# A gated mix of linear attention and eight experts: more rooms for the sums of the second layer's weights, and another order of the steps of the queries

## The chip, the cores and the metric

The kernel runs on one core of one Trainium2 chip. The metric is the device time of one execution in microseconds (us), the median of several runs. Times of single instructions come from one profiled execution.

## The reference, cut to what matters

```python
x = A_x                                             # 1 x 2048 x 512
g = sigmoid((x * gate_w).sum(-1, keepdims=True))
a = A_ref(x, A_wqkv, A_wo)
b = B_ref(x, B_w_gate, B_w1, B_w2)
return g * a + (1 - g) * b

def A_ref(x, wqkv, wo):                             # 32 heads of 16
    q, k, v = split_heads(x @ wqkv)
    phi = lambda t: where(t > 0, t + 1, exp(t)) + 1e-6
    pq, pk = phi(q), phi(k)
    kv = einsum("bhsd,bhse->bhde", pk, v)
    z = einsum("bhsd->bhd", pk)
    num = einsum("bhqd,bhde->bhqe", pq, kv)
    den = einsum("bhqd,bhd->bhq", pq, z)[..., None] + 1e-6
    return merge_heads(num / den) @ wo

def B_ref(x, w_gate, w1, w2):                       # 8 experts, hidden width 1792, all 8 are taken
    gates = softmax(x @ w_gate)
    return sum(gates[:, e] * (silu(x @ w1[e]) @ w2[e]) for e in range(8))
```

## The kernel before, in words

Every float32 operand of a matmul is split in a high part (a copy by ScalarE into the type the matmul rounds to) and a low part (VectorE: the value minus the high part). `mm3` (L56) multiplies high by high, high by low and low by high: lines 57, 58 and 59 are these three matmuls everywhere. `act_copy` (L61) is the copy by ScalarE; all such copies have line 62. `split` (L224) is the copy and the subtraction, one after the other. Both matmuls of an expert are computed by a scheme of seven products of halves in place of eight, so sums and differences of blocks of the inputs, of the weights and of the hidden values are made first.

The program has three stages.

**Keys.** The keys' features and the sums with the values are gathered over all 2048 rows. It ends with `normaliser`, `drain`, `state`, `gates` and `fold`, which give the matrix `wph`, `wpl` (state times `wo`, high and low).

**Queries.** The rows are in four blocks s = 0 to 3 of 512; each block has four slices c = 0 to 3 of 128 features.
- `q_proj(s, c)` (L414) makes 12 matmuls into a bank "a" of PSUM (there are two), then `phi`: an exponential on ScalarE (L320) and two steps of VectorE (L321, L322). Then it splits the result into `un`.
- `q_sums(s)` (L429), after the four slices of a block, makes 12 matmuls into bank "b" (one bank), a copy by ScalarE, one reciprocal of 32 x 512 by VectorE (L436), and the split into `rh`.
- `q_norm(s, c)` (L440) spreads the reciprocals over the features by two matmuls into bank "c" (one bank), multiplies by them on VectorE (L445), and splits the product into `hl`.
- `a_out(s, c)` (L449) makes 12 matmuls of `hl` with `wph` and `wpl` into four banks "dn"; after the last slice ScalarE copies them out (L461), and they are stored.
- `x_sums(p, step)` (L515) makes, for half p of the rows, four sums of blocks of x on VectorE (steps 0 to 3, 128 x 1024 each) and splits them (steps 4 to 7). For p = 1 the parts are stored to DRAM (`xstash`).

The blocks overlap: block s is projected while block s - 2 is normalised and put out. Near the end the first group of expert weights is loaded (`m.load`) and prepared (`m.prep`).

**Experts.** A group g is 256 of the hidden units of an expert; there are 112 groups (two halves of the rows, eight experts, seven groups each). `up(g, k, ...)` (L634), k = 0 to 6, makes the seven products of a group, six matmuls each, into banks "a", "b", "c". `prep(g + 1, k)` (L130) at the same time prepares the next group's weights: the first layer's go into tiles `o`; the second layer's (sums included) go into tiles `ws`, four to a group and two rooms in all, and are stored to DRAM (`w2stash`, seven stores a group, L183 and L158). The raw weights `rm` come in four loads a group into two rooms (L117, L120). From step u = LAG = 44 on, `tick(n)` (L803) adds the second layer: six matmuls more in each step. Its hidden operands are tiles `ho` (five rooms), its weights come back from `w2stash`.

The order on each engine is the order of the code: nothing is scheduled by a tool. An instruction waits on its engine until its inputs are there and its room is free, and everything behind it on that engine waits with it. Loads and stores are issued in order on SP's queue, but for some on GpSimd's.

The whole order of the queries is at L537 to L585.

Of the kernel before, what the change touches and what calls it, by code (L numbers as in the profile page):

```python
# [16 lines left out]
P = 128  # L17
# [19 lines left out]
def f32(ap):  # L37
    return ap.bitcast(F32)
# [57 lines left out]
def weights(m):  # L96
# [5 lines left out]
    m.ORDER = ("P1", "P7", "P2", "P4", "P6", "P5", "P3")  # L102
    raw, ops, ws = {}, {}, {}
    m.ops = ops


    def raw_tile(name):
# [22 lines left out]
    def prep(g, step):  # L130
# [12 lines left out]
        def low(i, src):  # L143
            o = ops[g][i][0]
            v.tensor_sub(two(o, 1), src, f32(two(o, 0)))  # L145

        def high2(n, src):
            if both:
                w = ws[g, n] = o_tile(f"ws{g}_{n}", "ws", 2, D)
                act_copy(two(w, 0), src)  # L150

        def low2(n, src, *prods):
            if both:
# [13 lines left out]
        elif step == 1:  # L167
# [2 lines left out]
            act_copy(o[:, 0], r[:, 1, 1, 0])  # L170
            ops[g][6] = o, 0
            if both:
                w = ws[g, 0] = o_tile(f"ws{g}_0", "ws", 2, D)
                act_copy(w[:, 0, :HALF], r[:, 0, 0, 1])
            high2(1, r[:, :, 1, 1])
        elif step == 2:
            o = ops[g][6][0]
# [28 lines left out]
def attention(m):  # L206
# [207 lines left out]
    def q_proj(s, c):  # L414
        tb = TBO[s]
        cs = slice(c * P, (c + 1) * P)
        ps = m.ps_tile(f"q{s}{c}", "a")
        for k in range(KT):
            nc.tensor.matmul(ps, wqh[:, k, cs], xk(0, tb, k), start=(k == 0), stop=False)
            nc.tensor.matmul(ps, wqh[:, k, cs], xk(1, tb, k), start=False, stop=False)  # L420
        for k in range(KT):
            nc.tensor.matmul(ps, wql[:, k, cs], xk(0, tb, k), start=False, stop=(k == KT - 1))
        d = pq[s, c] = sf_tile(f"pq{s}{c}") if s in (0, 3) else scr[:, (s - 1) * KT + c, :]
        phi(d, ps)
        u = un[s, c] = o_tile(f"un{s}{c}")
        split(d, u[:, 0], u[:, 1])


    def q_sums(s):  # L429
        ps = m.ps_tile(f"dn{s}", "b")[:NH, :]  # L430
        for c in range(KT):
            u = un.pop((s, c))
            mm3(ps, zc[:, 0, c, :], zc[:, 1, c, :], u[:, 0], u[:, 1], c == 0, c == KT - 1)
        r = hid.tile([NH, TB], F32, name=f"r{s}", tag="r", bufs=1)
        nc.scalar.activation(r, ps, AF.Copy, bias=1e-6)
        v.reciprocal(r, r)  # L436
        rec[s] = hid.tile([NH, 2, TB], F32R, name=f"rh{s}", tag="rh", bufs=2)
        split(r, rec[s][:, 0], rec[s][:, 1])

    def q_norm(s, c):  # L440
        ps = m.ps_tile(f"n{s}{c}", "c")
        for j in range(2):
            nc.tensor.matmul(ps, spread[:, c, :], rec[s][:, j], start=(j == 0), stop=(j == 1))
        d = pq.pop((s, c))
        v.tensor_mul(d, d, ps)  # L445
        h = hl[s, c] = hl_tile(f"hl{s}{c}")
        split(d, h[:, 0], h[:, 1])

    def a_out(s, c):  # L449
        h = hl.pop((s, c))  # L450
# [64 lines left out]
    def x_sums(p, step):  # L515
        a, b = raw[2 * p], raw[2 * p + 1]
        b11, b21, b12, b22 = a[:, :2], a[:, 2:], b[:, :2], b[:, 2:]
        if step == 0:
            v.tensor_sub(b11, b12, b11)
        elif step == 1:  # L520
            v.tensor_sub(b12, b22, b12)
        elif step == 2:
            v.tensor_sub(b22, b22, b11)
        elif step == 3:
            v.tensor_sub(b21, b21, b22)
        else:
            i, r = ((1, b11), (3, b22), (5, b12), (6, b21))[step - 4]
            if p == 0:
                XO[0][i] = [x_tile(f"t{i}{c}") for c in "hl"]
                split(r, *XO[0][i])  # L530
            else:
                h, lo = hl_tile(f"t{i}h"), hl_tile(f"t{i}l")
                split(r, h, lo)
                for c, t in enumerate((h, lo)):
                    nc.sync.dma_start(m.xstash[step - 1, c], f32(t).rearrange("p k t -> p (k t)"))

    q_proj(0, 0)  # L537
    y_acc(NT - 1)
    normaliser()
    drain()  # L540
    q_proj(0, 1)
    state()
    gates()
    q_proj(0, 2)
    q_proj(0, 3)
    wph, wpl = fold()
    for c in range(KT):
        q_proj(1, c)
        if c == 0:
            q_sums(0)  # L550
        x_sums(1, c)
    for s in (2, 3):
        for c in range(KT):
            q_proj(s, c)
            if c == 0:
                q_sums(s - 1)
            q_norm(s - 2, c)
            if s == 2:
                x_sums(1, 4 + c)
            else:  # L560
                x_sums(0, c)
            if c > 0:
                a_out(s - 2, c - 1)
        if s == 2:
            load_x(0), load_x(1)
        a_out(s - 2, KT - 1)
    q_norm(2, 0)
    q_sums(3)
    for c in range(KT):
        if c:  # L570
            q_norm(2, c)
        x_sums(0, 4 + c)
        if c > 0:
            a_out(2, c - 1)
        if c == 2:
            m.load(0)
    q_norm(3, 0)
    a_out(2, KT - 1)
    m.load(1)
    for c in range(KT):  # L580
        if c + 1 < KT:
            q_norm(3, c + 1)
        m.prep(0, 2 * c)
        a_out(3, c)
        m.prep(0, 2 * c + 1)  # L585

    XO[0][0], XO[0][2], XO[0][4] = X[0, 0], X[0, 1], X[1, 1]
    nc.gpsimd.memset(m.ident, 1.0)
# [6 lines left out]
def experts(m):  # L595
# [132 lines left out]
    def high(n):  # L728
        if 0 <= n < NTICK:
# [1 line left out]
            if n % 6 == 5:  # L731
                h = m.xpool.tile([P, 2, TB], F32R, name=f"ho{n}", tag="xs", bufs=2)
            else:
                h = hp.tile([P, 2, TB], F32R, name=f"ho{n}", tag="ho", bufs=5)
            act_copy(h[:, 0], t[SRC[prod]])
            hop[n] = h, t[SRC[prod]]

# [140 lines left out]
    for u in range(LAG + NTICK):  # L878
# [107 lines left out]
```

## Time and profile before

| what | us |
|---|---|
| median of 3 runs (2427.65 to 2429.86) | 2428.75 |
| the profiled execution's own time | 2427.99 |
| its span, first to last instruction | 2426.2 |
| TensorE busy (PE) | 2384.3 |
| its weight loads (PEld), beside PE | 1956.8 |
| VectorE busy (DVE) | 1807.9 |
| ScalarE busy (ACT) | 1369.1 |
| GpSimd busy (POOL) | 135.0 |

Rows of the profile name the engine, the line, the operation, then output and inputs by the program's names, and the shape. `<-` behind an idle time names what ended it. "PEclk" or "granted clock" is TensorE's clock as a share of full speed. Matmuls overlap, so their pitch is read from their starts and not from their durations.

### The profile page before, as it was taken

The page shows a single profiled execution, that of the slowest core. Times are in us where ns is not written, and L with a number is a line of the kernel's source. Part 1 is how long each engine was busy: PE and PEld are TensorE (multiplying, and loading weights), DVE is VectorE, ACT ScalarE, POOL GpSimd, SP SyncE. Part 2 cuts the span into 40 slices and gives each one's busy share as a digit, 9 for nine tenths or more (in the row PEclk, how much of TensorE's full clock was granted, in tenths as well). Part 3 has the DMA queues.
Part 4 walks back from the last instruction along what each step waited for, and adds up shares of the span by engine and source line. Part 5 has one row for each costly group of instructions (what it writes and reads, how often), then busy time and mean ns, then how long its engine had stood idle before and what let it go on. Part 6 is the DMA issues. An engine that isn't in the chain of part 4 may idle for free.

```text
span 2426.2 us, 31298 instructions
## 1 busy us (share of the span) xinstructions
PE 2384.3 (98%) x10627; PEld 1956.8 (81%) x10627; DVE 1807.9 (75%) x3055; ACT 1369.1 (56%) x2545; POOL 135.0 (6%) x173
## 2 busy tenths in 40 slices
PE   8988899999999999999999999999999999999998
PEld 7865678888888888888888888888888888888887
DVE  6666688888888888888887667666766766666757
ACT  4343666666666666666655555555555555555543
POOL 2100100000000000000000000000000000000011
PEclk9999999999999999999999999999999999999999
DMA  4422788879888888889886544455454544445456
GB/s 146 149 96 96 233 272 261 284 255 280 260 267 271 264 278 260 269 266 284 263 261 236 147 157 155 161 165 161 148 160 134 150 139 142 142 142 156 134 171 225
DMA packets 295984, 487.66 MB, mean 201 GB/s; under 512 B 22416, under 2 KB 214032, under 8 KB 294672
## 3 DMA queue, kind: packets, MB, share of 16 engines
q1 hardware_dynamic: 278480, 453.09, 55.9%
q0 software_dynamic: 17344, 32.58, 7.8%
q8 instruction: 83, 1.36, 0.2%
q14 instruction: 77, 0.63, 0.1%
HBM read 334.52 MB, written 151.06 MB: 200 GB/s over the span
## 4 chain that ended last, share of the span: by engine, by line
PE 92%; DVE 3%; DMA 2%; ACT 1%; issue 1%; SPq 1%; DVEq 0%; ACTq 0%
PE p L57 15%; PE p L58 15%; PE p L59 15%; PE a L57 8%; PE a L59 8%; PE a L58 8%; PE c L58 4%; PE c L57 4%; PE c L59 4%; PE b L58 2%; PE b L57 2%; PE b L59 2%; PE g L329 1%; DMA w2stash<-ws 1%; DVE r L436 0%
## 5 line engine op out<-in xcount | busy, mean ns | idle before, releaser
L57 PE MATMUL p<-ho,w 128*128 128x512 f32 x1568 | 611.0, 390 | 1.5 <-DVE k L798 0.7
L58 PE MATMUL p<-ho,w 128*128 128x512 f32 x1568 | 610.0, 389 | 0.0
L59 PE MATMUL p<-ho,w 128*128 128x512 f32 x1568 | 610.0, 389 | 0.0
L741 DVE TENSOR_TENSOR ho<-s,ho 128x512 fp32r<-128x512 f32 x784 | 537.5, 687 | 60.8 <-ACT ho L62 58.3
L62 ACT ACTIVATE ho<-s 128x512 fp32r<-128x512 f32 x784 | 487.3, 622 | 18.9 <-PE p L59 12.7
L57 PEld LDWEIGHTS p<-ho,w 128*128 128x128 f32 x1568 | 294.3, 188 | 64.8 <-ACT p L62 1.8
L59 PEld LDWEIGHTS p<-ho,w 128*128 128x128 f32 x1568 | 294.4, 188 | 61.2
L58 PEld LDWEIGHTS p<-ho,w 128*128 128x128 f32 x1568 | 294.3, 188 | 60.8
L62 ACT ACTIVATE o<-rm 128x512 fp32r<-128x512 f32 x448 | 255.5, 571 | 149.5 <-PE a L59 124.6
L624 ACT ACTIVATE s<-s 128x512 f32<-128x512 f32 x224 | 141.7, 633 | 286.2 <-DVE s L683 208.2
L145 DVE TENSOR_TENSOR o<-rm,o 128x512 fp32r<-128x512 f32 x336 | 230.5, 686 | 14.4 <-ACT o L62 13.8
L683 DVE TENSOR_TENSOR s<-c,s 128x512 f32<-128x512 f32 x112 | 77.3, 690 | 168.1 <-PE c L59 164.5
L62 ACT ACTIVATE ws<-rm 128x256 fp32r<-128x256 f32 x224 | 126.7, 572 | 87.3 <-DMA w2stash<-ws 74.6
L690 DVE TENSOR_TENSOR s<-a,s 128x512 f32<-128x512 f32 x112 | 77.4, 691 | 74.1 <-PE a L59 73.5
L155 DVE TENSOR_TENSOR ws<-rm,ws 128x512 fp32r<-128x512 f32 x168 | 115.3, 687 | 20.5 <-ACT ws L62 18.9
L624 ACT ACTIVATE s<-b 128x512 f32<-128x512 f32 x112 | 67.3, 600 | 104.8 <-PE b L59 91.4
L62 ACT ACTIVATE s<-a 128x512 f32<-128x512 f32 x112 | 66.8, 597 | 91.2 <-PE a L59 91.2
L178 DVE TENSOR_TENSOR o<-rm,o 128x256 fp32r<-128x256 f32 x112 | 47.2, 422 | 64.2 <-ACT o L62 63.9
L775 POOL DMA_DIRECT2D acct<-c x28 | 24.2, 864 | 1093.5 <-DVE c L771 650.1
L62 ACT ACTIVATE s<-c 128x512 f32<-128x512 f32 x112 | 66.7, 596 | 26.7 <-PE c L59 26.7
L713 DVE TENSOR_TENSOR s<-s,s 128x512 f32<-128x512 f32 x112 | 77.0, 688 | 0.0
L722 DVE TENSOR_TENSOR s<-s,s 128x512 f32<-128x512 f32 x112 | 77.0, 687 | 0.0
(334 smaller groups left out, 4471.7 us busy)
## 6 DMA issues: line engine op xcount, KB each, us to landing
w<-w2stash SPq DMA_DIRECT2D x392, 512.0 KB, 4.3
w2stash<-ws SPq DMA_DIRECT2D x392, 256.0 KB, 4.7
rm<-wm SPq DMA_DIRECT2D x336, 256.0 KB, 4.8
wb<-wgtd SPq DMA_DIRECT2D x16, 512.0 KB, 5.7
x<-xT SPq DMA_DIRECT2D x7, 1024.0 KB, 6.2
acct<-c POOLq DMA_DIRECT2D x28, 256.0 KB, 5.7
acct<-d POOLq DMA_DIRECT2D x28, 256.0 KB, 5.7
acct<-k POOLq DMA_DIRECT2D x26, 256.0 KB, 5.4
```

Source lines behind the costliest of these rows:

```text
L57: nc.tensor.matmul(ps, wh, xh, start=start, stop=False, skip_group_check=True)
L58: nc.tensor.matmul(ps, wh, xl, start=False, stop=False, skip_group_check=True)
L59: nc.tensor.matmul(ps, wlo, xh, start=False, stop=stop, skip_group_check=True)
L62: nc.scalar.activation(dst, src, AF.Copy)
L145: v.tensor_sub(two(o, 1), src, f32(two(o, 0)))
L155: v.tensor_sub(two(w, 1), src, f32(two(w, 0)))
L624: nc.scalar.activation(dst, src, AF.Silu)
L683: v.tensor_add(sn[g, 2], bank[g, "c"], sn[g, 2])
L690: v.tensor_add(sn[g, 3], bank[g, "a"], sn[g, 3])
L713: v.tensor_sub(t12, t22, t12)
L722: v.tensor_sub(t21, t21, t11)
L741: v.tensor_sub(h[:, 1], s, f32(h[:, 0]))
```

## The change

Six things are changed.

1. `q_proj` no longer splits. The copy (`q_high`) and the subtraction (`q_low`) are functions of their own, so are those of `q_norm` (`n_high`, `n_low`) and those of the x splits (`x_high`, `x_low`); the order of the queries places them one by one.
2. The reciprocal of a block is made in four quarters of 32 x 128 (`q_rec`), one in each slice of the next block; the split of it follows as `q_rec_split`.
3. `q_norm` takes bank "c" for even slices and bank "b" for odd ones.
4. The x sums and splits stand at other places: two sums of half 1 are made during block 0, the splits of half 1 during the first two slices of block 2; the sums of half 0 during block 3, its splits from there into the remainder. The order of the splits is 3, 5, 1, 6 in place of 1, 3, 5, 6.
5. The loads of x blocks 0 and 1 come after the third slice of block 2, those of the weight groups 0 and 1 after slices 1 and 3 of the remainder.
6. In the experts, until step 35, the first three of a group's four `ws` tiles are taken from the five rooms of `ho` (named `wx` there); before, and from step 36 on, they are from the two rooms of `ws`.

The core of the diff:

```diff
+        def ws_tile(n):
+            w = ws[g, n] = m.spare(f"wx{g}_{n}") if m.spare and n < 3 else o_tile(f"ws{g}_{n}", "ws", 2, D)
+            return w
+
         def high2(n, src):
             if both:
-                w = ws[g, n] = o_tile(f"ws{g}_{n}", "ws", 2, D)
-                act_copy(two(w, 0), src)
+                act_copy(two(ws_tile(n), 0), src)
...
         phi(d, ps)
-        u = un[s, c] = o_tile(f"un{s}{c}")
-        split(d, u[:, 0], u[:, 1])
+
+    def q_high(s, c):
+        un[s, c] = o_tile(f"un{s}{c}")
+        act_copy(un[s, c][:, 0], pq[s, c])
+
+    def q_low(s, c):
+        u = un[s, c]
+        v.tensor_sub(u[:, 1], pq[s, c], f32(u[:, 0]))
...
+    def q_rec(s, i):
+        r = rec[s][:, i * P:(i + 1) * P]
         v.reciprocal(r, r)
-        rec[s] = hid.tile([NH, 2, TB], F32R, name=f"rh{s}", tag="rh", bufs=2)
+
+    def q_rec_split(s):
+        r, rec[s] = rec[s], hid.tile([NH, 2, TB], F32R, name=f"rh{s}", tag="rh", bufs=2)
         split(r, rec[s][:, 0], rec[s][:, 1])
 
     def q_norm(s, c):
-        ps = m.ps_tile(f"n{s}{c}", "c")
+        ps = m.ps_tile(f"n{s}{c}", "cb"[c % 2])
...
-    q_proj(0, 2)
-    q_proj(0, 3)
+    q_step(0, 2)
+    x_sums(1, 0)
+    q_step(0, 3)
+    x_sums(1, 1)
     wph, wpl = fold()
     for c in range(KT):
         q_proj(1, c)
         if c == 0:
             q_sums(0)
-        x_sums(1, c)
+        q_high(1, c)
+        q_rec(0, c)
+        q_low(1, c)
+        if c in (1, 3):
+            x_sums(1, 2 + c // 2)
+    q_rec_split(0)
     for s in (2, 3):
         for c in range(KT):
             q_proj(s, c)
             if c == 0:
                 q_sums(s - 1)
             q_norm(s - 2, c)
-            if s == 2:
-                x_sums(1, 4 + c)
-            else:
-                x_sums(0, c)
+            q_high(s, c)
+            n_high(s - 2, c)
+            if s == 2 and c < 2:
+                x_high(1, 2 * c)
+            q_low(s, c)
+            n_low(s - 2, c)
+            q_rec(s - 1, c)
+            if s == 2 and c < 2:
+                x_low(1, 2 * c)
+                x_high(1, 2 * c + 1)
+                x_low(1, 2 * c + 1)
...
-        if s == 2:
-            load_x(0), load_x(1)
+            if s == 2 and c == 2:
+                load_x(0), load_x(1)
+        q_rec_split(s - 1)
         a_out(s - 2, KT - 1)
-    q_norm(2, 0)
     q_sums(3)
     for c in range(KT):
-        if c:
-            q_norm(2, c)
-        x_sums(0, 4 + c)
+        q_norm(2, c)
+        n_high(2, c)
+        if c < 2:
+            q_rec(3, 2 * c)
+        x_low(0, c) if c == 1 else None
+        n_low(2, c)
+        if c < 2:
+            q_rec(3, 2 * c + 1)
+        if c == 1:
+            m.load(0)
+            q_rec_split(3)
...
+    def ho_tile(name):
+        return hp.tile([P, 2, TB], F32R, name=name, tag="ho", bufs=5)
...
+        m.spare = ho_tile if u < LAG - 8 else None
```

Three places show how instructions move on their engines. Line numbers of the changed kernel are higher: L325 and L326 are there what L321 and L322 are before (`phi`), L436 and L468 are the low parts of `un` and `hl`, L449 the quarter of a reciprocal, L460 the product with the spread reciprocals (L445 before), L540 to L546 the four x sums (L519 to L525 before), L558 the low parts of the x splits.

VectorE at the start of block s = 1, before: `q10`, `q11` are the projections of slices 0 and 1, `r0` the sums of block 0, `rh0` its split reciprocals, `x2`, `x3` raw x.

```order
L321 TENSOR_SCALAR scr_300<-scr_300 128x512
L322 SCALAR_TENSOR_TENSOR scr_300<-q10_1414,scr_300 128x512
L226 TENSOR_TENSOR un10_1430<-scr_300,un10_1430 128x512
L436 RECIPROCAL r0_1446<-r0_1446 32x512
L226 TENSOR_TENSOR rh0_1449<-r0_1446,rh0_1449 32x512
L519 TENSOR_TENSOR x2_1244<-x3_1251,x2_1244 128x1024
L321 TENSOR_SCALAR scr_300<-scr_300 128x512
L322 SCALAR_TENSOR_TENSOR scr_300<-q11_1453,scr_300 128x512
```

The same place on VectorE, now:

```order
L325 TENSOR_SCALAR scr_300<-scr_300 128x512
L326 SCALAR_TENSOR_TENSOR scr_300<-q10_1416,scr_300 128x512
L449 RECIPROCAL r0_1445<-r0_1445 32x128
L436 TENSOR_TENSOR un10_1447<-scr_300,un10_1447 128x512
L325 TENSOR_SCALAR scr_300<-scr_300 128x512
L326 SCALAR_TENSOR_TENSOR scr_300<-q11_1451,scr_300 128x512
```

Between the two slices stood a whole reciprocal, its split and an x sum; now a quarter of a reciprocal stands there, between the slice's phi and its low part.

VectorE at the start of block s = 2, before: `n00` and `n01` are the spread reciprocals of block 0, `pq00` its features, `t1l` the low part of an x split.

```order
L322 SCALAR_TENSOR_TENSOR scr_300<-q20_1513,scr_300 128x512
L226 TENSOR_TENSOR un20_1529<-scr_300,un20_1529 128x512
L436 RECIPROCAL r1_1545<-r1_1545 32x512
L226 TENSOR_TENSOR rh1_1548<-r1_1545,rh1_1548 32x512
L445 TENSOR_TENSOR pq00_1276<-pq00_1276,n00_1551 128x512
L226 TENSOR_TENSOR hl00_1555<-pq00_1276,hl00_1555 128x512
L226 TENSOR_TENSOR t1l_1559<-x2_1244,t1h_1558 128x1024
L321 TENSOR_SCALAR scr_300<-scr_300 128x512
```

The same place on VectorE, now:

```order
L326 SCALAR_TENSOR_TENSOR scr_300<-q20_1516,scr_300 128x512
L460 TENSOR_TENSOR pq00_1276<-pq00_1276,n00_1547 128x512
L436 TENSOR_TENSOR un20_1551<-scr_300,un20_1551 128x512
L468 TENSOR_TENSOR hl00_1553<-pq00_1276,hl00_1553 128x512
L449 RECIPROCAL r1_1545<-r1_1545 32x128
L558 TENSOR_TENSOR t3l_1556<-x3_1251,t3h_1555 128x1024
L558 TENSOR_TENSOR t5l_1565<-x3_1251,t5h_1564 128x1024
L325 TENSOR_SCALAR scr_300<-scr_300 128x512
```

The product with the spread reciprocals follows phi at once, each low part has another row between it and the step that its copy needs, and two x splits stand where one stood.

ScalarE in the preparation of weight group 2, before: `ws2_0` to `ws2_3` are the four tiles of sums of the second layer's weights, `s1_1` to `s4_0` what leaves the banks of TensorE.

```order
L62 ACTIVATE ws2_0_2319<-rm2_2190 128x256
L62 ACTIVATE ws2_1_2321<-rm2_2190 128x512
L624 ACTIVATE s4_0_2330<-a0_2197 128x512
L62 ACTIVATE s3_1_2342<-c1_2335 128x512
L624 ACTIVATE s1_1_2355<-b1_2314 128x512
L62 ACTIVATE o2_2_2359<-rm2_2190 128x512
L62 ACTIVATE s2_1_2367<-a1_2307 128x512
L62 ACTIVATE ws2_2_2370<-rm2_2190 128x512
```

The same place on ScalarE, now:

```order
L62 ACTIVATE wx2_0_2331<-rm2_2202 128x256
L62 ACTIVATE wx2_1_2333<-rm2_2202 128x512
L704 ACTIVATE s4_0_2342<-a0_2209 128x512
L62 ACTIVATE s3_1_2354<-c1_2347 128x512
L704 ACTIVATE s1_1_2367<-b1_2326 128x512
L62 ACTIVATE o2_2_2371<-rm2_2202 128x512
L62 ACTIVATE s2_1_2379<-a1_2319 128x512
L62 ACTIVATE wx2_2_2382<-rm2_2202 128x512
```

The order is the same; the tiles are in other rooms, and only the group's fourth is still in one of the two of `ws`.

More of the change, by code (lines that the diff above doesn't have):

```diff
@@ L104, in weights @@
     m.ops = ops
+    m.spare = None
     def raw_tile(name):
@@ L172, in prep @@
             if both:
-                w = ws[g, 0] = o_tile(f"ws{g}_0", "ws", 2, D)
-                act_copy(w[:, 0, :HALF], r[:, 0, 0, 1])
+                act_copy(ws_tile(0)[:, 0, :HALF], r[:, 0, 0, 1])
             high2(1, r[:, :, 1, 1])
@@ L526, in x_sums, with x_high, x_low, q_step @@
         else:
[L527 to L530, printed above, removed]
-            else:
[L532 to L537, printed above, removed]
+            n, low = divmod(step - 4, 2)
+            i, r = ((3, b22), (5, b12), (1, b11), (6, b21))[n]
+            if not low:
+                if p == 0:
+                    XO[0][i] = [x_tile(f"t{i}{c}") for c in "hl"]
+                else:
+                    tmp[i] = hl_tile(f"t{i}h"), hl_tile(f"t{i}l")
+                act_copy((tmp[i] if p else XO[0][i])[0], r)
+            else:
+                h, lo = tmp[i] if p else XO[0][i]
+                v.tensor_sub(lo, r, f32(h))
+                if p:
+                    for c, t in enumerate((h, lo)):
+                        nc.sync.dma_start(m.xstash[{1: 3, 3: 4, 5: 5, 6: 6}[i], c], f32(t).rearrange("p k t -> p (k t)"))
+    tmp = {}
+    def x_high(p, n):
+        x_sums(p, 4 + 2 * n)
+    def x_low(p, n):
+        x_sums(p, 5 + 2 * n)
+    def q_step(s, c):
+        q_proj(s, c)
+        q_high(s, c)
+        q_low(s, c)
+    q_step(0, 0)
     y_acc(NT - 1)
@@ L540, in attention @@
     drain()
-    q_proj(0, 1)
+    q_step(0, 1)
     state()
     gates()
-    q_proj(0, 2)
-    q_proj(0, 3)
+    q_step(0, 2)
+    x_sums(1, 0)
+    q_step(0, 3)
+    x_sums(1, 1)
     wph, wpl = fold()
@@ L557, in attention @@
             q_norm(s - 2, c)
-            if s == 2:
-                x_sums(1, 4 + c)
-            else:
-                x_sums(0, c)
+            q_high(s, c)
+            n_high(s - 2, c)
+            if s == 2 and c < 2:
+                x_high(1, 2 * c)
+            q_low(s, c)
+            n_low(s - 2, c)
[4 more added lines that the diff above has]
+                x_low(1, 2 * c + 1)
+            if s == 3:
+                if c < 3:
+                    x_sums(0, c)
+                if c == 2:
+                    x_sums(0, 3)
+                    x_high(0, 0)
+                if c == 3:
+                    x_low(0, 0)
+                    x_high(0, 1)
             if c > 0:
                 a_out(s - 2, c - 1)
-        if s == 2:
-            load_x(0), load_x(1)
+            if s == 2 and c == 2:
+                load_x(0), load_x(1)
+        q_rec_split(s - 1)
         a_out(s - 2, KT - 1)
-    q_norm(2, 0)
     q_sums(3)
     for c in range(KT):
-        if c:
-            q_norm(2, c)
-        x_sums(0, 4 + c)
+        q_norm(2, c)
[9 more added lines that the diff above has]
+            q_rec_split(3)
+        if c in (1, 2):
+            x_high(0, c + 1)
+        if c in (2, 3):
+            x_low(0, c)
         if c > 0:
             a_out(2, c - 1)
-        if c == 2:
-            m.load(0)
+        if c == 3:
+            m.load(1)
     q_norm(3, 0)
+    n_high(3, 0)
+    n_low(3, 0)
     a_out(2, KT - 1)
-    m.load(1)
     for c in range(KT):
+        m.prep(0, 2 * c)
         if c + 1 < KT:
             q_norm(3, c + 1)
-        m.prep(0, 2 * c)
+            n_high(3, c + 1)
+            n_low(3, c + 1)
+        m.prep(0, 2 * c + 1)
         a_out(3, c)
-        m.prep(0, 2 * c + 1)
     XO[0][0], XO[0][2], XO[0][4] = X[0, 0], X[0, 1], X[1, 1]
@@ L733, in high @@
             else:
-                h = hp.tile([P, 2, TB], F32R, name=f"ho{n}", tag="ho", bufs=5)
+                h = ho_tile(f"ho{n}")
             act_copy(h[:, 0], t[SRC[prod]])
```

12 lines of the change are left out of this document (8 added, 4 removed).

## The prediction

> **What bounds the kernel now.** I read the page's slices first, then windows cut at the kernel's stages, then the waits and the rows of single engines inside the two stages with holes.
>
> ```profile
> PE   8988899999999999999999999999999999999998
> ```
>
> This is TensorE's busy share in 40 slices of 60.7 us. TensorE carries the span; what can be won lies in the first six slices. The windows cut them: start and end, length, then busy time and instructions (x) of PE, PEld, DVE, ACT, POOL, the granted clock, DMA share and GB/s.
>
> ```profile
> 122.62:140.32 17.70, 15.57 (x62) 11.16 (x61) 13.73 (x17) 6.08 (x12) 0.00 (x0) 0.93 0.00 1
> 140.32:176.12 35.80, 30.96 (x118) 21.32 (x117) 25.67 (x32) 15.44 (x24) 0.00 (x0) 0.94 0.26 104
> 176.12:210.72 34.60, 31.28 (x119) 21.17 (x117) 20.88 (x26) 11.87 (x20) 0.00 (x0) 0.95 0.33 116
> 210.72:248.27 37.55, 33.65 (x123) 22.44 (x123) 25.36 (x33) 16.53 (x28) 0.00 (x0) 0.91 0.38 124
> 248.27:330.07 81.80, 69.73 (x268) 51.59 (x267) 58.13 (x96) 52.51 (x102) 8.37 (x16) 0.94 0.79 251
> 332.00:2300.00 1968.00, 1968.00 (x8715) 1630.62 (x8714) 1498.31 (x2545) 1163.04 (x2174) 85.07 (x99) 1.00 0.67 209
> ```
>
> The four first rows are the queries (query block s=1, s=2, s=3, and the remainder after the last projection), the fifth is the start of the experts until the second layer's first product, the last is the rest. There TensorE has no idle time, one matmul every 1968/8715 = 0.226 us; the edit does not touch that loop, so I leave the rest as it is. In the queries (125.65 us in four rows) TensorE has holes and a lower clock. The waits of TensorE in those four rows:
>
> ```profile
> PE n L443 <- DVE scr L445: 6.3, 2, 3.9
> PE n L443 <- DVE pq L445: 3.9, 1, 3.9
> PE q L419 <- DVE scr L322: 2.1, 1, 2.1
> PE a L57 <- ACT hl L62: 1.9, 2, 1.0
> ```
>
> These are microseconds in total, times, longest: 14.2 us in six waits, four of them over 2 us. The named releaser is DVE's product that empties bank c, or its phi that empties a bank of "a". What a long hole costs behind itself stands in TensorE's rows (start, duration, instruction, idle before it in brackets):
>
> ```profile
> 187.82 0.73 PE L443 MATMUL n<-rh,spread 32*128 32x512 f32 x2 [2.41 <-DVE scr L445]
> ...
> 190.23 0.63 PE L58 MATMUL a<-wpl,hl 128*128 128x512 f32 x1
> ...
> 193.11 0.39 PE L419 MATMUL q<-x00h,wqh 128*128 128x512 f32 x1
> 193.34 0.40 PE L420 MATMUL q<-x00l,wqh 128*128 128x512 f32 x1
> ```
>
> After the hole matmuls last 0.63 us in place of 0.39 and start about 0.43 apart, later again 0.23. A hole under 1 us does not do that:
>
> ```profile
> 172.98 0.50 PE L57 MATMUL a<-wph,hl 128*128 128x512 f32 x1 [0.96 <-ACT hl L62]
> ...
> 174.04 0.40 PE L57 MATMUL a<-wph,hl 128*128 128x512 f32 x1
> 174.27 0.39 PE L58 MATMUL a<-wpl,hl 128*128 128x512 f32 x1
> ```
>
> Why DVE was late is in DVE's own rows at the start of s=3:
>
> ```profile
> 182.46 3.34 DVE L436 RECIPROCAL r<-r 32x512 f32<-32x512 f32 x1
> 186.49 0.68 DVE L226 TENSOR_TENSOR rh<-r,rh 32x512 fp32r<-32x512 f32 x1 [0.69 <-ACT rh L62]
> 187.10 0.67 DVE L445 TENSOR_TENSOR scr<-scr,n 128x512 f32<-128x512 f32 x1
> 188.47 0.69 DVE L226 TENSOR_TENSOR hl<-scr,hl 128x512 fp32r<-128x512 f32 x1 [0.70 <-ACT hl L62]
> 189.08 1.22 DVE L519 TENSOR_TENSOR x<-x,x 128x1024 f32<-128x1024 f32 x1
> 190.21 0.42 DVE L321 TENSOR_SCALAR pq<-pq 128x512 f32<-128x512 f32 x1
> 190.67 0.69 DVE L322 SCALAR_TENSOR_TENSOR pq<-q,pq 128x512 f32<-128x512 f32 x1
> ```
>
> The reciprocal of 3.34 us stands ahead of the product at 187.10 that TensorE's second spreading needs, and each split makes DVE wait 0.7 us for ScalarE's copy. DVE's largest group of waits over the queries:
>
> ```profile
> DVE hl L226 <- ACT hl L62: 11.9, 16, 0.8
> ```
>
> **Queries, step by step.** First the floor. A matmul of 512 columns costs 0.23 us (starts at 193.11 and 193.34). A spreading pair costs more:
>
> ```profile
> 161.41 0.62 PE L422 MATMUL q<-x31h,wql 128*128 128x512 f32 x2
> 161.97 0.73 PE L443 MATMUL n<-rh,spread 32*128 32x512 f32 x2
> 162.63 0.50 PE L57 MATMUL a<-wph,hl 128*128 128x512 f32 x1
> 162.96 0.39 PE L58 MATMUL a<-wpl,hl 128*128 128x512 f32 x1
> ```
>
> The last projection row ends its two starts at 161.41 + 0.46 = 161.87; the second output matmul starts at 162.96, so the pair takes 1.09 - 0.23 = 0.86 us. By the code s=1 has 60 matmuls, s=2 and s=3 have 108 and four pairs each, the remainder 108 and eight pairs: 13.8, 28.3, 28.3 and 31.7 us, together 102.1. Of the 125.65 us thus 23.5 are to be had at most: 14.2 in the waits and 9.3 in slow matmuls, 2.3 for each of the four long holes.
>
> Next DVE's load. The quarters' price is not in the trace; it lies between a proportional share, 3.34/4 = 0.84, and a whole 3.34. A narrow reciprocal is:
>
> ```profile
> 116.17 0.25 DVE L498 RECIPROCAL gat<-gat 128x16 f32<-128x16 f32 x1
> ```
>
> 512 columns take 3.34 and 16 take 0.25, so 6.2 ns a column and 0.15 fixed; 128 columns give 0.95, which I take, since the row of 16 shows how small the fixed part is. Sixteen quarters make 15.2 us against 13.4: 1.8 more on DVE, beside TensorE except in s=1. With phi at 1.06 (0.46 from start to start, then 0.6 as rows overlap), product and low part at 0.61 to 0.67, and the 1024-wide steps at 1.13 to 1.22, DVE has 13.4 us in s=1, 20.8, 21.8, and 25.4 in the remainder. Only in s=1 is that TensorE's own amount. So the stages are TensorE's, provided nothing stands in a row's way. I went through the new rows in order with these durations:
>
> - s=1: DVE needs 1.06 + 0.95 + 0.61 + half of 1.2 = 3.2 us an iteration against TensorE's 2.8, with a head start of one bank: TensorE waits 0.5 for the fifth projection. 14.3 us. Two 1.2 us sums moved ahead of it make phi(1,0) about 0.9 late, which the two banks hide.
> - s=2: 0.4 wait for the split of the reciprocals (low part behind the last x-sum), 0.6 for the last output operand: 29.3. The four x splits now stand in the first two iterations, 2.5 us of DVE each; projections two banks ahead hide them. Their DMAs come earlier on SP's queue, and the loads of x0, x1 behind them come some 15 us earlier than now; nothing else stands there. The loads of weight groups 0 and 1 likewise stand ahead of block 2's stores, the first some 13 us before its use, and land in 5.0.
> - s=3: no wait found, 28.3.
> - Remainder: the quarters of the last block, the last x splits and the first weight group's preparation fall here. Waits of 1.5 (first output operand behind a quarter), 0.6, 0.7 and 1.3 (last operand behind two weight sums): 35.8.
>
> Sum 107.7, so the queries give **18.0 us**; bounds 23.5 (no wait) and 12 (a third of it lost to semaphores and to one or two long holes left). That the ScalarE copy now runs while DVE does another row is where the 0.7 us waits go; the bank "b" for every second spreading removes the wait for the previous product, and adds one: the spreading must follow ScalarE's reading of the sums in "b", 0.6 us, which the next projection covers except in the remainder (in the 1.5), where only the output products stand behind it.
>
> [...] Holes of 0.96 us stayed at 0.23 us a matmul and one of 2.41 did not, so a slowdown of 2.3 us behind 1.5 cannot be excluded. [...]
>
> **Start of the experts.** Waits of ScalarE, DVE and TensorE from 248.27 to 330.07:
>
> ```profile
> ACT ws L62 <- DMA w2stash<-ws: 20.3, 11, 4.9
> ...
> DVE ws L155 <- ACT ws L62: 17.5, 9, 5.1
> ...
> PE c L57 <- ACT s L62: 4.5, 4, 3.6
> PE a L57 <- DVE s L690: 3.8, 4, 2.2
> PE a L57 <- ACT s L62: 3.6, 6, 0.7
> ```
>
> ScalarE waits for a room of "ws" until a store has landed, DVE waits for ScalarE, and both then empty TensorE's banks late. The stretch has 265 matmuls and a small transposition: 265 x 0.229 + 0.45 = 61.1 us, so 20.7 of 81.8 are to be had. A group of 42 matmuls needs 9.6 us; (81.8 us hold 6.3 groups) now it takes about 12.5. What is late next is DVE. A group's rows from one dense stretch, first and last:
>
> ```profile
> 297.40 0.69 DVE L186 TENSOR_TENSOR rm<-rm 128x512 f32<-128x512 f32 x1
> ...
> 305.81 0.42 DVE L181 TENSOR_TENSOR ws<-rm,ws 128x256 fp32r<-128x256 f32 x1
> ```
>
> Fifteen rows in 8.8 us, 0.3 of it a wait, and the group's third ws row at 0.7 missing: 9.2 us against 9.6. It fits, barely. The rooms: seven in place of two; a sum stays 5 us (0.6 copy, 0.7 low part, issue, 3.2 to land) and up to 9 where rows stand between copy and low part, four sums a group, so rooms no longer bind until prep of group 6, which has two again. The DMAs:
>
> ```profile
> w2stash<-ws SPq DMA_DIRECT2D x46, 256.0 KB, 3.2
> rm<-wm SPq DMA_DIRECT2D x26, 256.0 KB, 5.0
> ```
>
> Eleven transfers a group are 2.9 MB, 300 GB/s at 9.6 us, above the 251 of the window. The four loads are issued about 1.5 to 4 us into a group behind DVE's last sum, land 5.0 later, and are used from 9.6 on: about a microsecond to spare. I add 0.45 us a group for four groups (between 0 and the present 2.9; nearest to the dense rows), 0.7 in the first, where ScalarE loads its table, and 2.5 where two rooms are back. 66.1 us: **15.7 us** saved; bounds 20.7, and 6 if the loads become the bound.
>
> **Sum.** The profiled execution took 2427.99 (span 2426.2 and 1.8 around it). 2427.99 - 18.0 - 15.7 = 2394.3; the median of the runs is 0.76 higher, so 2395.
>
> **Rivals.**
> - *Loads become the wait* in the start of the experts: groups at 11.5 us in place of 10.1, six of them, 9 us: 2404. For it: 300 GB/s and a microsecond to spare; against: the 251 GB/s is a mean with all of ScalarE's 20.3 us of waits in it, so it is no ceiling. Chance 0.15.
> - *Short holes slow the clock*: six holes left in the queries at 2.3 each: 2409. Against it the 0.96 us hole. 0.10.
> - *Quarters cost by the call*, 3.34 each: DVE gets 38 us more, its stages 23, 30, 31 and 35 become the bound, the queries give 2: 2411. The 0.25 us row speaks against it. 0.03.
> - *The rooms do not free the copy*, because the spare rooms lie in memory of the query stage and first wait for its last stores: one wait of some 4 us and two long holes behind it, 9 us: 2404. 0.04.
> - *Slower*: the stores, no longer held back by rooms, crowd out the loads of raw weights. Each microsecond by which a group outgrows 10.1 costs 6.3; it decides from 15.4 us a group (33 us given back), 188 GB/s. At 17 us: 2438. The 251 GB/s already reached speak against it. 0.02.
> - *Almost all waits go*: 2387. 0.09.
>
> **How the numbers follow.** Forecast 2395 with 0.57; the rivals as given. The range 2385 to 2410 reaches from both upper bounds (2428.75 - 44.2) to both lower ones (2428.75 - 18) and leaves out the quarters by the call, the slower case and the edges, under 0.2. A measurement of this kernel tells 0.2% from no change, 4.9 us: faster 0.95, same 0.03, slower 0.02.
>
> **What would show it.** Right: the four query rows sum to about 108 us with at most one TensorE hole over 2 us and a clock near 1; reciprocals of 128 columns at 0.9 to 1.0; no ScalarE wait for w2stash between the first group and group 6; second layer's first product near 296; the loop after it unchanged. Wrong: DVE waits for raw weights in every group, slow matmuls behind holes near 1 us, or a changed rate in the long loop.

## The result, and the profile after

| | before | after |
|---|---|---|
| median, us (4 runs each, measured together) | 2428.77 (2427.65 to 2429.86) | 2390.41 (2390.03 to 2390.54) |
| profiled execution, us | 2427.99 | 2390.3 |
| its span, us | 2426.2 | 2388.5 |
| TensorE busy, us | 2384.3 | 2369.8 |
| queries, first product of s = 1 to first of the experts, us | 125.65 | 106.56 |
| start of the experts, to the second layer's first product, us | 81.80 | 63.82 |

The ratio is 0.9842 (95% interval 0.9825 to 0.9859): 38.4 us less, with 2395 forecast and 2385 to 2410 as the range. Of the 37.7 us between the two profiled executions 19.1 are in the queries, 18.0 in the start of the experts, and 0.75 are already there when s = 1 begins (121.87 in place of 122.62).

The page of the changed kernel, TensorE's 40 slices (here of 59.7 us), has lost the eights of its third to fifth slices:

```profile
PE   8999999999999999999999999999999999999998
```

Windows of the changed kernel, cut at the same matmuls as those of before (s = 1, s = 2, s = 3, the remainder, the start of the experts, then a stretch of the long loop); the columns are start and end, length, busy time and instructions of PE, PEld, DVE, ACT and POOL, the granted clock, DMA share, GB/s. One pair of matmuls, the spreading of block 2's first slice, is counted in s = 3 in the rows of before and in the remainder here (some 0.7 us), since it now stands behind the sums of block 3:

```profile
121.87:136.22 14.35, 14.32 (x62) 10.29 (x60) 11.52 (x18) 6.13 (x11) 0.00 (x0) 1.00 0.00 1
136.22:164.70 28.48, 28.48 (x117) 20.21 (x117) 25.91 (x37) 15.34 (x24) 0.00 (x0) 1.00 0.56 222
164.70:193.30 28.60, 28.60 (x118) 19.94 (x116) 21.48 (x30) 12.56 (x21) 0.00 (x0) 1.00 0.10 37
193.30:228.43 35.13, 33.92 (x126) 22.14 (x125) 24.87 (x37) 17.26 (x30) 0.00 (x0) 0.95 0.43 146
228.43:292.25 63.82, 61.49 (x269) 49.66 (x267) 56.76 (x93) 50.83 (x99) 8.41 (x16) 1.00 0.98 320
294.00:2262.00 1968.00, 1968.00 (x8714) 1630.26 (x8714) 1497.88 (x2544) 1163.39 (x2174) 85.07 (x99) 1.00 0.67 209
```

In s = 2 and s = 3 busy time equals length: TensorE does not wait at all there. In the remainder 1.2 us are idle and the clock is 0.95; in the start of the experts 2.3 us are idle at a full clock. The long loop is what it was: 8714 matmuls in 1968 us, 8715 before. The idle time by what ended it, first the queries, then the start of the experts:

```profile
PE a L57 <- ACT hl L62: 1.2, 2, 0.7
```

```profile
PE a L57 <- ACT s L62: 0.9, 2, 0.7
PE c L57 <- ACT s L62: 0.9, 1, 0.9
PE a L57 <- DVE s L770: 0.5, 1, 0.5
```

Before there were 14.2 us in six waits in the queries alone. Of ScalarE's 20.3 us of waits for the store `w2stash` in the start of the experts one is left:

```profile
ACT ws L62 <- DMA w2stash<-ws: 2.5, 1, 2.5
```

VectorE's rows at the start of s = 2 in the changed kernel (start, duration, instruction) show the pieces side by side: a quarter is 0.93 us, the next row starts 0.86 later, and no row waits for the copy of the row before it.

```profile
138.60 0.93 DVE L449 RECIPROCAL r<-r 32x128 f32<-32x128 f32 x1
139.46 0.68 DVE L436 TENSOR_TENSOR un<-scr,un 128x512 fp32r<-128x512 f32 x1
140.05 1.22 DVE L546 TENSOR_TENSOR x<-x,x 128x1024 f32<-128x1024 f32 x1
141.19 0.67 DVE L230 TENSOR_TENSOR rh<-r,rh 32x512 fp32r<-32x512 f32 x1
```

Its largest waits over the queries were 11.9 us for the copies of `hl`; that group is now

```profile
DVE hl L468 <- ACT hl L62: 4.4, 6, 0.8
```

The one place with slow matmuls that is left, TensorE's rows in the remainder:

```profile
196.15 1.47 PE L458 MATMUL n<-rh,spread 32*128 32x512 f32 x4
198.32 0.50 PE L57 MATMUL a<-wph,hl 128*128 128x512 f32 x1 [0.70 <-ACT hl L62]
198.66 0.40 PE L58 MATMUL a<-wpl,hl 128*128 128x512 f32 x1
199.06 0.80 PE L59 MATMUL a<-wph,hl 128*128 128x512 f32 x1
199.65 0.63 PE L57 MATMUL a<-wph,hl 128*128 128x512 f32 x1
...
202.21 0.47 PE L57 MATMUL a<-wph,hl 128*128 128x512 f32 x1
202.52 0.39 PE L58 MATMUL a<-wpl,hl 128*128 128x512 f32 x1
```

A hole of only 0.70 us, and behind it steps of 0.43 us from 199.65 on, until 202.2. The eight steps from 199.06 to 202.52 take 3.46 us; where these rows are not slowed (e1_rooms_off, below) they take 1.94, so TensorE loses 1.5 us to the clock (granted 0.95 over the remainder, 1.00 in e1_rooms_off). That is less than the prediction's 2.3 for a long hole, but it is behind a short one, which the prediction took to be free.

### The profile page after: what moved, and what is told of

Its sections match the earlier page's. It is cut to its first block, busy times and chain, and to the rows that moved or that the text cites. A ratio compares the mean times of both kernels' runs of the same rounds, so it can differ in the third digit from the quotient of the medians.

```text
span 2388.5 us, 31289 instructions
## 1 busy us (share of the span) xinstructions
PE 2369.8 (99%) x10627; PEld 1951.1 (82%) x10627; DVE 1805.4 (76%) x3067; ACT 1368.6 (57%) x2545; POOL 135.1 (6%) x173
## 4 chain that ended last, share of the span: by engine, by line
PE 96%; DVE 2%; ACT 1%; DMA 1%; issue 0%; SPq 0%; DVEq 0%; ACTq 0%
PE p L57 15%; PE p L59 15%; PE p L58 15%; PE a L57 9%; PE a L59 9%; PE a L58 9%; PE c L59 4%; PE c L57 4%; PE c L58 4%; PE b L59 2%; PE b L58 2%; PE b L57 2%; PE g L333 1%; PE q L426 1%; PE q L423 1%; PE q L424 1%
## 5 line engine op out<-in xcount | busy, mean ns | idle before, releaser
L62 ACT ACTIVATE ws<-rm 128x512 fp32r<-128x512 f32 (+1 forms) x209 | 118.4, 573 | 67.9 <-DMA w2stash<-ws 61.1
L160 DVE TENSOR_TENSOR ws<-rm,ws 128x512 fp32r<-128x512 f32 x158 | 108.4, 686 | 3.2 <-DMA rm<-wm 2.5
```

The costliest lines, as they stand in the source:

```text
L62: nc.scalar.activation(dst, src, AF.Copy)
L160: v.tensor_sub(two(w, 1), src, f32(two(w, 0)))
```

## The experiments

The two parts can be made without each other, so the first two kernels do one each; the next four take single edits out of the changed kernel; the last five vary the rooms, look for what is left and repeat the changed kernel. "Queries" and "start" are the two stretches of the table above, cut at the same matmuls. The diff also turns round the order within the last four slices (a step of the first weight group's preparation now stands ahead of each next spreading); the list of six changes does not name this, and no kernel here undoes it alone.

| kernel | median us (4 runs; the last 5) | ratio to before, 95% | queries | start |
|---|---|---|---|---|
| e1_rooms_off | 2405.80 | 0.9906 (0.9888 to 0.9923) | 106.29 | 78.85 |
| e2_rooms_only | 2411.52 | 0.9928 (0.9912 to 0.9943) | 125.50 | 64.77 |
| e3_one_bank | 2389.97 | 0.9840 (0.9825 to 0.9856) | 106.30 | 63.42 |
| e4_whole_rec | 2394.53 | 0.9859 (0.9843 to 0.9874) | 110.83 | 63.87 |
| e5_splits_together | 2395.19 | 0.9860 (0.9844 to 0.9877) | 111.51 | 63.70 |
| e6_x_old_places | 2392.69 | 0.9849 (0.9835 to 0.9864) | 109.30 | 63.36 |
| e7_one_sum_moved | 2402.41 | 0.9889 (0.9874 to 0.9904) | 106.28 | 75.64 |
| e8_norm_first | 2389.64 | 0.9836 (0.9822 to 0.9851) | 105.89 | 63.84 |
| e9_rooms_longer | 2388.42 | 0.9835 (0.9822 to 0.9848) | 106.36 | 60.98 |
| e10_both_more | 2387.88 | 0.9834 (0.9820 to 0.9847) | 105.89 | 60.98 |
| e11_changed_again | 2390.65 | 0.9845 (0.9831 to 0.9858) | 106.57 | 63.87 |

**One part at a time.** The changed kernel with the `ws` tiles in their two rooms throughout:

```diff
-        m.spare = ho_tile if u < LAG - 8 else None
+        m.spare = None
```

> The changed kernel with all sums of the second layer's weights back in the two rooms of ws; the new order of the queries is kept. Theory (the two parts add, and the rooms alone carry the start of the experts): that stretch goes from 63.8 us back to 81 to 82, the queries stay at 106.6, and the time is 2408 to 2409. Rival (the earlier weight loads of the new order help that stretch too): it grows by 12 us or less, 2402 or below.

2405.8 (2404.8 to 2406.6), between theory and rival. The start has nearly all its old length, 78.85 of 81.80, and the old waits, of TensorE first, then of ScalarE:

```profile
PE a L57 <- DVE s L770: 7.2, 4, 3.6
PE c L57 <- ACT s L62: 3.1, 3, 1.7
```

```profile
ACT ws L62 <- DMA w2stash<-ws: 15.7, 8, 4.7
```

So the rooms are what shortens the start. The 3 us by which it is shorter without them are not a shorter wait, as its window shows beside the fifth row of before:

```profile
228.09:306.94 78.85, 65.69 (x269) 49.91 (x268) 56.64 (x93) 50.86 (x99) 8.38 (x16) 0.98 0.82 259
```

TensorE idles 13.2 us here and 12.1 before, but is busy 65.69 us in place of 69.73, at a clock of 0.98 in place of 0.94: before, both holes of over 2 us (3.56 and 2.16 us) have slow matmuls behind them, here one of two (last section). And the queries gain their 19 us without the rooms.

The other way round, the queries as before and only the rooms new (the rest of the diff undone):

> The kernel before with the spare rooms alone. Theory: the queries stay at 125.6 us, the start of the experts goes from 81.8 to 64 us, and the time is 2410 to 2411. Rival (without the earlier loads the raw weights come too late once rooms no longer hold ScalarE up): the stretch stays above 69 us, and the time is 2416 or more.

2411.5 (2410.1 to 2412.6), half a microsecond above the theory's range, with the stretches it expected: start 64.77, and the queries' waits are those of before to the tenth (6.3, 3.9, 2.1 and 1.9 us). The two kernels are 22.6 and 16.9 us below the kernel before that ran with them; their sum, 39.4, is close to the 38.4 of both together. The two parts add up and do not help each other.

**The second bank.** Every spreading in bank "c":

```diff
-        ps = m.ps_tile(f"n{s}{c}", "cb"[c % 2])
+        ps = m.ps_tile(f"n{s}{c}", "c")
```

> The changed kernel with every spreading in bank c again. Theory of the prediction's words (the second bank removes TensorE's wait for the previous product, which the profile of before names with 10.2 us in three waits): several us come back, 2394 to 2400. Rival (the product was late because of the reciprocal ahead of it on VectorE; with that gone, bank c is empty in time): 2390 to 2391.5, with one short wait more in the remainder at most.

2389.97 (2389.87 to 2390.71): nothing lost. The wait that the bank was to remove is there, in the remainder alone and small:

```profile
PE n L458 <- DVE scr L460: 1.1, 2, 0.8
PE a L57 <- ACT hl L62: 0.7, 1, 0.7
```

There are no slow matmuls behind it. Two kernels below that keep the second bank and have none either, e1_rooms_off and e7_one_sum_moved, have the same queries (106.29 and 106.28 us), so the bank is worth nothing at an equal clock either. The three waits of before that named this product (10.2 us, two on `scr` and one on `pq`) are gone here with one bank: it is enough that the reciprocal no longer stands ahead of the product on VectorE. What a second bank would have done in the old order was not run.

**Quarters or a whole.** One reciprocal of 32 x 512 where the first quarter stands, the other three left out:

```diff
     def q_rec(s, i):
-        r = rec[s][:, i * P:(i + 1) * P]
-        v.reciprocal(r, r)
+        if i == 0:
+            v.reciprocal(rec[s], rec[s])
```

> The changed kernel with each block's reciprocal made whole, 3.3 us, at the place of its first quarter. Theory (quarters matter only where the next output operand stands right behind them, in the remainder): queries 3 to 6 us longer, all of it behind the last block's reciprocal, 2393 to 2397. Rival (a whole reciprocal brings a hole of TensorE and a slow stretch in every block, as before): 12 us or more, 2402 and up.

2394.5 (2393.9 to 2395.5), 4.1 above the changed kernel. The queries are 4.3 longer: 3.0 in the remainder and 1.2 in the three stages before it, where the theory had expected none. In the remainder it is one hole, where the low part of the first output operand stands behind 3.34 us of reciprocal:

```profile
200.25 0.40 PE L58 MATMUL a<-wpl,hl 128*128 128x512 f32 x1
203.05 0.80 PE L59 MATMUL a<-wph,hl 128*128 128x512 f32 x1 [2.40 <-DVE hl L468]
203.64 0.63 PE L57 MATMUL a<-wph,hl 128*128 128x512 f32 x1
```

In s = 1 to s = 3 the whole reciprocal at its new place, behind phi and the products, makes TensorE wait 0.8 us in all. So the quarters are worth 4 us, most of it one hole of 2.4 with its slow matmuls. That the rest of the old reciprocal's harm lay in its place is argued from VectorE's rows; no kernel puts it back there.

**Copy and low part together.** The splits as before, at the places of the copies:

```diff
     def q_high(s, c):
-        un[s, c] = o_tile(f"un{s}{c}")
-        act_copy(un[s, c][:, 0], pq[s, c])
+        u = un[s, c] = o_tile(f"un{s}{c}")
+        split(pq[s, c], u[:, 0], u[:, 1])
...
     def q_low(s, c):
-        u = un[s, c]
-        v.tensor_sub(u[:, 1], pq[s, c], f32(u[:, 0]))
+        pass
```

and the same for `n_high` and `n_low`.

> The changed kernel with copy and low part of un and hl one right after the other again; quarters, banks and places of the x steps are kept. Theory (VectorE's waits of 0.7 us for ScalarE's copies were off the path where TensorE has more to do than VectorE): about 12 us of such waits come back on VectorE over the queries, of which s=1 and the remainder show 2 to 4 us: 2392 to 2395. Rival (these waits were what made VectorE late): 7 us or more, 2397 and up, with holes in s=2 and s=3.

2395.2 (2394.3 to 2397.1): 4.8 above, the queries 5 us longer. VectorE waits again, 6.3 and 4.3 us for the copies of `hl` and `un`, and TensorE's waits in the queries rise from 1.2 to 4.0 us, none of them over 0.82:

```profile
PE a L57 <- ACT hl L62: 2.1, 3, 0.7
PE q L423 <- DVE scr L326: 0.8, 1, 0.8
PE n L457 <- ACT rh L62: 0.6, 1, 0.6
PE n L457 <- DVE rh L230: 0.5, 1, 0.5
```

Most of the other 2 us are slow matmuls behind such short holes, in two places (from 145.4 and from 203.4). The place was not the expected one: 2.9 of the 5 us are in s = 2 (31.35 us in place of 28.48), 0.8 in s = 1 and 1.3 in the remainder. Holes in s = 2 were the rival's sign, at less than its price.

**The x steps at their old places**, one a slice in s = 1 and s = 2, the sums of half 0 in s = 3 and its splits in the remainder; the loads of x after s = 2:

```diff
-        if c in (1, 3):
-            x_sums(1, 2 + c // 2)
+        x_sums(1, c)
...
-            if s == 2 and c < 2:
-                x_low(1, 2 * c)
-                x_high(1, 2 * c + 1)
-                x_low(1, 2 * c + 1)
+            if s == 2:
+                x_low(1, c)
             if s == 3:
...
+                x_sums(0, c)
```

> The changed kernel with the x sums and splits back at their old places: four sums in s=1, one split in each slice of s=2, one sum in each slice of s=3, all four splits of half 0 in the remainder. Theory: s=1, where VectorE and TensorE are level, gets 2.3 us more of VectorE and the remainder one split of 1.2 more: 3 to 5 us with what a hole slows behind it, 2393 to 2396. Rival (the banks hide it all): 2390 to 2391.5.

2392.7 (2392.1 to 2394.2), 2.3 above, between theory and rival: the queries are 2.7 longer, 2.2 of it in the remainder, where four splits of x now stand among the output products, and 0.5 in s = 2 and s = 3; s = 1, where the theory had seen the cost, is unchanged at 14.35. This is a small term.

Taken out one at a time, the four edits thus give back -0.3, 4.3, 5.0 and 2.7 us of the queries, 11.7 of the 19.1. What the other 7 hang on, the reciprocal's place or edits that stand in for each other, was not separated.

**How many rooms.** Only one of a group's four sums goes to the rooms of `ho`; three share the two of `ws`:

```diff
-            w = ws[g, n] = m.spare(f"wx{g}_{n}") if m.spare and n < 3 else o_tile(f"ws{g}_{n}", "ws", 2, D)
+            w = ws[g, n] = m.spare(f"wx{g}_{n}") if m.spare and n < 1 else o_tile(f"ws{g}_{n}", "ws", 2, D)
```

> The changed kernel with only the first of a group's four ws tiles in the spare rooms; three are left to the two rooms of ws. Theory (a tile holds its room 6 to 7 us until its store has landed, so three tiles in two rooms need about 10 us a group against 9.5): the start of the experts grows by 2 to 6 us, 2392 to 2396. Rival (one tile out of the way is enough): 2390 to 2391.5. Second rival (two rooms for three tiles are as bad as for four): 2402 and up.

2402.4 (2401.9 to 2403.7): the second rival. Only 3.2 of the 15 us between e1_rooms_off and the changed kernel are kept, and ScalarE waits nearly as long as with all four in two rooms (15.7 there):

```profile
ACT ws L62 <- DMA w2stash<-ws: 14.9, 7, 3.7
```

ScalarE's rows in one group show how. The two rooms are taken in turn, so the copy at 256.26 and the copy at 266.69, of the group's second and fourth sum, have the same room:

```profile
256.26 0.62 ACT L62 ACTIVATE ws<-rm 128x512 fp32r<-128x512 f32 x1
...
266.69 0.63 ACT L62 ACTIVATE ws<-rm 128x512 fp32r<-128x512 f32 x1 [3.55 <-DMA w2stash<-ws]
```

It was held 10.4 us, longer than the 9.5 of a group that does not wait: the second sum's stores are issued at 259.24 and 260.21, and their landing ends ScalarE's wait. With three sums moved 2.5 us of it are left, with this one 14.9: it does not shrink in proportion.

**What is left.** The first spreading of the remainder ahead of the sums of s = 3, where it stood in the kernel before, so that the hole at 198.3 falls away:

```diff
+    q_norm(2, 0)
+    n_high(2, 0)
     q_sums(3)
     for c in range(KT):
-        q_norm(2, c)
-        n_high(2, c)
+        if c:
+            q_norm(2, c)
+            n_high(2, c)
+        else:
+            n_low(2, 0)
...
-        n_low(2, c)
+        if c:
+            n_low(2, c)
```

> The changed kernel with the first spreading of block 2 ahead of the sums of block 3 in the remainder, so that its product and split are made while TensorE makes the sums; the last block's first quarter comes behind that split. Theory (the hole of 0.7 us there and the slow matmuls behind it cost what they last): 0.5 to 2.5 us less than the changed kernel, 2388 to 2390. Rival (the spreading must wait for the split of block 2's reciprocals, and the hole moves ahead of it): 2390 to 2391.

2389.6 (2389.2 to 2390.4), 0.8 below the changed kernel's first median, with ranges that overlap; the hole moved and did not go:

```profile
197.50 0.73 PE L458 MATMUL n<-rh,spread 32*128 32x512 f32 x2 [0.74 <-ACT r L445]
```

Now the second spreading needs the bank of the sums, which ScalarE reads (the wait that bank "b" brings). No slow matmuls followed here, and the queries are 0.7 us shorter. Less than half of it is the clock: e1_rooms_off has the changed kernel's order in the queries and no slow matmuls either, and is only 0.3 shorter (106.29), because its later waits for `hl` are longer (0.34 and 0.73 in place of none and 0.49), and the gaps too short for the list of waits are too. TensorE makes up most of the 1.5 us in the changed kernel by waiting less.

The rooms of `ho` taken for four more steps, for two sums a group:

```diff
-            w = ws[g, n] = m.spare(f"wx{g}_{n}") if m.spare and n < 3 else o_tile(f"ws{g}_{n}", "ws", 2, D)
+            w = ws[g, n] = m.spare(f"wx{g}_{n}") if m.spare and n < m.spares else o_tile(f"ws{g}_{n}", "ws", 2, D)
...
-        m.spare = ho_tile if u < LAG - 8 else None
+        m.spare = ho_tile if u < LAG - 4 else None
+        m.spares = 3 if u < LAG - 8 else 2
```

> The changed kernel, but in the first-layer steps 36 to 39 the first two of a group's four sums still go to the rooms of ho. Theory (ScalarE's two waits for rooms at group 6, 2.5 us and about as much in the next group, are nearly all hidden, since TensorE stays 99% busy there): 2389.5 to 2391, first product of the second layer within 0.5 us of 292.25. Rival (those waits still reach TensorE): 2387 to 2389, first product at 289 to 291. Second rival (rooms of ho taken this late hold up the first hidden operands of the second layer): 2392 or more, with TensorE or ScalarE waits on ho after 292.

2388.4 (2387.2 to 2389.5). The rival is right and my theory wrong: ScalarE's waits for rooms at group 6 were not hidden. The second layer's first product comes at 289.42, and the windows of this kernel show the start of the experts without idle time:

```profile
228.44:289.42 60.98, 60.86 (x269) 49.73 (x267) 56.56 (x93) 50.97 (x99) 8.38 (x16) 1.00 1.00 327
```

Both edits at once, and the changed kernel again beside them:

> The rooms kept longer, and in the remainder the product with the spread reciprocals moved ahead of the sums (together). Theory (only the second does something, 0.5 to 1 us, by the hole and the slow matmuls behind it): 2389 to 2390, the queries' four rows 105.5 to 106.2 us and the start of the experts as in the changed kernel, 63.8. Rival (both do): 2387 to 2388.8, start 62 to 63. Second rival (none): 2390 to 2391.

> The changed kernel once more, on the same chip as the two variants: 2389.9 to 2391. It also shows whether the hole of 0.70 us in the remainder, at the same rows, is followed by matmuls 0.43 us apart each time (theory of a fixed cause) or only in some executions (rival: 1.5 to 2 us less between 196 and 228 us where it is not).

2387.9 (2387.5 to 2388.9) against 2390.65 (2389.9 to 2391.8) on the same chip: every run of the first is below every run of the second, by 2.8 us in the medians. That is 0.1%. It is the lowest median here, though the runs of e9_rooms_longer overlap with it. Both edits do something, as the rival had it, and the first by more than it said: the start is that of e9_rooms_longer, 60.98, and its queries are those of e8_norm_first, 105.89, still 3.8 above the floor of 102.1. The changed kernel's second profile has the slow matmuls again, at another moment (last section).

## Why the prediction was right, and where it was not

The forecast and its two halves held: 18.0 forecast and 19.1 measured in the queries, 15.7 and 18.0 in the start of the experts, 2395 and 2390.4 in all. Point by point:

- **The quarter** was taken at 0.95 us from the rows of 512 and of 16 columns; it is 0.93 to 0.94. VectorE indeed bounds nothing: in s = 2 it is busy 25.9 of 28.5 us and TensorE does not wait. The 20.8 forecast for that stage was too low for what runs in it: the row at 140.05 is an x sum of s = 1.
- **The stages** were forecast at 14.3, 29.3, 28.3 and 35.8 us and measured at 14.35, 28.48, 28.60 and 35.13. The floors (13.8, 28.3, 28.3, 31.7) carry this. The holes of 0.4 and 0.6 in s = 2 are not there, nor the 0.5 for the fifth projection in s = 1.
- **The remainder** came out near its number by other parts. Four waits of 4.1 us were forecast; there are two, 0.70 and 0.49. The first output operand does stand behind a quarter, but only its low part, which the third matmul needs: the first two cover it, and the hole ends with ScalarE's copy. In place of the missing waits there are 1.5 us of slow matmuls that the sum did not have. That is still 3.4 above the floor of 31.7; gaps too short for the list of waits make up the rest. The sum has no slow matmuls behind its wait of 1.5 us; that was my estimate, and no row of before showed it, whose holes in the queries and the start of the experts are of up to 1.03 us or from 2.13 on. The runs show both cases: none behind the hole of 1.41 us in e6_x_old_places, some behind the one of 0.70 here.
- **The second bank** is the step that brought nothing. "The bank "b" for every second spreading removes the wait for the previous product": e3_one_bank has that wait back, 1.1 us in all, and no later end. It was read from the name of a releaser, while the product was late behind a reciprocal. That bank "b" adds a wait for ScalarE's reading was right in kind: it is the 0.74 us in e8_norm_first.
- **The start of the experts** was mis-sized in its small terms. 0.45 us a group for four groups and 0.7 in the first (its table load is a row of ScalarE of 1.28 us, at 258.46 before) are nothing: in e9_rooms_longer the whole stretch is 60.98 us with the floor at 61.1. The 2.5 us where two rooms are back was right: 63.82 - 60.98 = 2.8. So the forecast's 66.1 was 2.3 too long by terms that I had put in between a bound of 0 and one of 2.9.
- **Loads as the wait** (the first rival) did not come. The DMA share is 0.98 at 320 GB/s, above the 300 that I had worked out, and TensorE's waits name no load; with the rooms kept longer it is 1.00 at 327, and still none.
- **Short holes slow the clock** (the second rival, 2.3 us for each of six) came once, not six times, and for 1.5 us of which the end kept some 0.3. Its condition, the hole's length, was not the right one, and neither was it for the long holes: in e1_rooms_off one of 2.33 us stayed without slow matmuls (last section).
- Rooms that free nothing, quarters that cost by the call and the slower case are excluded by the rows: ScalarE waits once, the quarters are 0.93, and a group takes 9.52 us. The price of the second of these did not follow from its own stages: 23, 30, 31 and 35 us add up to 119, so the queries would have given 6.6 us and not 2, which makes 2406 in place of 2411. The forecast does not hang on it.
- The 0.75 us ahead of s = 1 were not forecast. They are no larger than the scatter: the kernel with only the rooms, unchanged up to there, begins s = 1 at 122.25, and kernels with the changed order up to there begin it between 121.62 and 122.47.

## What to carry to other kernels

A wait's releaser names what came last, not what was missing: look at what stands ahead of it on its own engine before you give it a buffer (here three waits, 10.2 us in all, named the product that empties bank "c", and with that one bank the changed kernel ran 2389.97 us, in place of 2390.41 with two). Where a slow row stands matters more than how long it is: here a full reciprocal of 3.34 us cost 1.2 us in three stages of four, with the urgent rows ahead of it, and 3.0 in the fourth alone, where they were not. For a buffer that is held until a store lands, count the time for which it is held, from the first copy into it to the landing of its last store (10.4 us in the group shown), times the sums made in it: ScalarE waited 14.9 us with three sums in two rooms, 15.7 with four, and 2.5 with one, at group 6.

## What had not been expected of the hardware

**A hole, short or long, may or may not slow the clock.** The changed kernel, profiled a second time (e11_changed_again), has the same hole at the same row and a later fall:

```profile
198.36 0.50 PE L57 MATMUL a<-wph,hl 128*128 128x512 f32 x1 [0.71 <-ACT hl L62]
...
199.66 0.39 PE L58 MATMUL a<-wpl,hl 128*128 128x512 f32 x1
199.89 0.56 PE L59 MATMUL a<-wph,hl 128*128 128x512 f32 x1
200.24 0.63 PE L57 MATMUL a<-wph,hl 128*128 128x512 f32 x1
```

The slow steps begin 1.5 us behind the hole here, 0.7 behind it in the first profile, and at once in e9_rooms_longer (198.55). In e1_rooms_off, whose rows there are the same, they do not come at all:

```profile
198.26 0.50 PE L57 MATMUL a<-wph,hl 128*128 128x512 f32 x1 [0.69 <-ACT hl L62]
...
200.03 0.39 PE L57 MATMUL a<-wph,hl 128*128 128x512 f32 x1
200.25 0.39 PE L58 MATMUL a<-wpl,hl 128*128 128x512 f32 x1
```

And a hole of twice the length, in e6_x_old_places, costs nothing behind itself:

```profile
227.94 0.50 PE L57 MATMUL a<-wph,hl 128*128 128x512 f32 x1 [1.41 <-ACT hl L62]
...
229.00 0.39 PE L57 MATMUL a<-wph,hl 128*128 128x512 f32 x1
229.23 0.39 PE L58 MATMUL a<-wpl,hl 128*128 128x512 f32 x1
```

Nor is a hole of over 2 us always followed by slow steps. In the start of the experts of e1_rooms_off:

```profile
266.64 0.50 PE L57 MATMUL a<-t6h,o 128*128 128x512 f32 x1 [2.33 <-DVE s L770]
266.98 0.39 PE L58 MATMUL a<-t6l,o 128*128 128x512 f32 x1
```

One of 2.10 us in e7_one_sum_moved (at 244.17) stayed fast too, while one of 2.16 us in the kernel before (at 290.29) has slow steps from 291.62 on.

The moment of the onset thus moves between executions, and the slow stretches differ in length: 3.15 us in the first profile (199.06 to 202.21), 5.15 behind the hole of 3.90 us before (221.28 to 226.43). The granted clock of the remainder is 0.95 in both profiles of the changed kernel and in e9_rooms_longer, and 1.00 in e1_rooms_off. No length of the hole divides the cases: slow steps follow 2.40 us in e4_whole_rec and 0.70 here, and none follow 2.33 in e1_rooms_off. The holes of under 1 us that were followed by slow steps all stood behind the twelve matmuls into `dn`, which use 32 columns, and the spreadings, which use 32 rows; the one of 1.41 us did not. But other holes at that place stayed fast (0.69 us in e1_rooms_off, 0.70 in e7_one_sum_moved), and no kernel was run that changes only what stands ahead of the hole: what decides it stays open.

**The DMA engines can be busy all the time without TensorE waiting for them.** A share of 1.00 at 327 GB/s over 61 us, in which TensorE idles 0.1 us, was reached in e9_rooms_longer. What is loaded there is used a group later; that distance was not varied.
